# Four layers in one launch: moving comparisons of the Fourier matrices between stages

## The chip, the cores and the metric

The kernel runs on one core of a Trainium2 chip. The metric is the device time of one execution in microseconds; of several runs the median is given. Engines are named as in the profile: PE multiplies matrices (PEld loads its weights), DVE, ACT and POOL work elementwise, SP issues all transfers of this kernel.

## The reference

Four layers follow one another on x of 2048 rows and 640 columns: attention, Fourier, attention, Fourier, each added to its input after a layer norm.

```python
x = A_x
x = x + _A_ref(_layernorm(x, axis=-1), A_wqkv, A_wo)
x = x + _B_ref(_layernorm(x, axis=-1), B_dft_seq_re, B_dft_seq_im, B_dft_hid_re, B_dft_hid_im)
x = x + _A_ref(_layernorm(x, axis=-1), A_wqkv, A_wo)
x = x + _B_ref(_layernorm(x, axis=-1), B_dft_seq_re, B_dft_seq_im, B_dft_hid_re, B_dft_hid_im)
```

`_A_ref` is attention with 32 heads of 20 columns, in which a row sees itself and the 255 rows before it. `_B_ref` is the real part of a transform along the columns and along the rows:

```python
a = jnp.einsum("bsd,ed->bse", x, dft_hid_re)
b = jnp.einsum("bsd,ed->bse", x, dft_hid_im)
y = jnp.einsum("ts,bse->bte", dft_seq_re, a) - jnp.einsum("ts,bse->bte", dft_seq_im, b)
```

The four matrices are inputs.

## The kernel before, in words

All is in float32, with products of the attention's weights split into a high and a low part. The order of all instructions is fixed when the program is built; each engine takes its own in that order, and an instruction that waits holds up all behind it on its engine.

**The comparisons.** The Fourier layers use the symmetries of cosine and sine matrices and multiply only with a small part of each. That the matrices given have these symmetries is tested on the chip: 180 pieces of the four matrices (`all_checks`, L1468) are compared with their mirrored parts, and the sum of the squared differences decides at the end (`judge`, L1541, and a branch at L1719) whether a general version of the whole network is run too; with these inputs it isn't. One comparison (`check`, L1494) is a load by SP of 128 rows of 456 numbers (428 for the first 18 pieces) into a spare buffer (L1501), one or two additions or subtractions (L1508) on POOL or DVE, and a square with a sum on ACT (L1512); after every eighth, DVE adds up eight sums (L1517). A buffer is loaded again when its square is done. The comparisons have no place of their own: they are woven into the stages of the four layers.

**The stages.** Each attention has a *prologue* (`before_heads`, L411): rows are normalized and turned by PE (`prep`), the columns of V are made for 16 tiles of 128 rows (`value`, L464), and the first columns of Q and K (`pieces`). In it a comparison is loaded by `check()` and its work is put down three comparisons later (`check_step`). Five buffers, `ou` and `rr`, go round. Then come the *heads* (`heads`, L652): 128 steps, in each of which PE makes the scores and the product with V of one block of 128 rows and four heads, beside parts of the projections. In steps 0 to 80, `IN_HEADS` = 12 comparisons are spread (L875); POOL and ACT do their parts some slots after the load. The heads' step also turns the row maxima and sends them by a transfer, `qp<-mt` (L695), to the operands of the next scores.

**The Fourier layer** (`fourier`, L1314) is first a *sequence product* (the loop over `PRODUCTS`, L1368) with four comparisons to a product on DVE and ACT, and then a *column product* (L1447): eight iterations, in each of which PE multiplies one tile (`straight`), ACT copies one of the two results (L1421), DVE adds and subtracts, and PE reverses the rows of the tile before (`turned`, L1436), after which DVE adds that too and SP stores both. For the tile `j == 0` ACT copies a row into each of the two operands first (L1434). `spread(n, again)` (L1342) sets comparisons beside this: it puts the squares of the ones taken in the iteration before on ACT, loads those buffers again, and gives the POOL parts of the next n. In the second Fourier layer it takes four an iteration; in the first, none: the comparisons begun there end before the column product. Between the two products of the first layer, SP loads the weights of the second attention, five of `wv` (L378, `value_weights`) and two of `wqk` (L546, `load_chunk`); their splitting (`split_w`, L380 on ACT and L383 on POOL) is spread over the column product from its third iteration on.

Before the change the comparisons lie so: 16 in the first prologue, 12 in the first heads, 50 in the first Fourier layer, 22 in the second prologue, 12 in the second heads, 68 in the second Fourier layer.

Of the kernel before, what the change touches and what calls it, by code (L numbers as in the profile page):

```python
# [7 lines left out]
F32 = mybir.dt.float32  # L8
# [10 lines left out]
D = 640  # L19
# [31 lines left out]
PRODUCTS = [(n, c) for n in ("ce", "co", "so", "se") for c in range(3)]  # L51
SIGMA, WIDE = 513, 57
SCALED, MARGIN = 2.0 ** 40, 2.0 ** 12
IN_HEADS, CHECKED = 12, 81

CHUNKS = ((0, 16, 0, 8), (0, 16, 8, 16), (16, 24, 0, 16), (24, 32, 0, 16), (0, 32, 16, 20))

# [7 lines left out]
def cuts(ap, n):  # L65

    return [ap[:, i:i + n] for i in range(0, ap.shape[1] - n + 1, n)]
# [6 lines left out]
class Net:  # L74
    def __init__(self, nc, tc, ctx, a, ok=None):
        self.nc, self.tc, self.a = nc, tc, a
        self.general = ok is None
        const = ctx.enter_context(tc.tile_pool(name="const", bufs=1))
        self.ln = ctx.enter_context(tc.tile_pool(name="ln", bufs=5))
        self.slots = ctx.enter_context(tc.tile_pool(name="slots", bufs=1))  # L80
        psum = ctx.enter_context(tc.tile_pool(name="psum", bufs=1, space=PSUM))
        self.work = ctx.enter_context(tc.tile_pool(name="work", bufs=2))
        dram = ctx.enter_context(tc.tile_pool(name="dram", bufs=1, space=DRAM))

        self.banks = psum.tile([P, 8, 512], F32, name="banks")

        def fixed(name, cols, dt):
            return const.tile([P, cols], dt, name=name)

        self.ident = fixed("ident", P, F32)  # L90
        nc.sync.dma_start(self.ident, a["ident"])
        self.flip = fixed("flip", P, F32)
        nc.sync.dma_start(self.flip, a["flip"])
        self.mask = fixed("mask", 384, BF16)
        self.ones = const.tile([1, 128], F32, name="ones")
        nc.vector.memset(self.ones, 1.0)
        self.half = fixed("half", 1, F32)
        nc.vector.memset(self.half, -0.5)
        self.big = [None] * 4
        self.qp, self.kp = [None] * 2, [None] * 2  # L100

        self.qk = dram.tile([2, 2 * D, S], F32, name="qk_d")
        self.vd = dram.tile([NQ, P, NB, 96], F32, name="v_d")
        self.od = dram.tile([H, 32, S], F32, name="o_d")
        self.rd = dram.tile([NSB, H, 512], F32, name="r_d")
        self.xs = [dram.tile([S, D], F32, name=f"x_d{i}") for i in range(3)]
        self.turn = {}
        self.xn = {}
        self.first = True
        self.slot = None  # L110
        self.posted = {}
        self.lanes = {n: deque() for n in ("act", "dve", "pool")}
        self.heavy = []
        self.owed = {}
        self.left = 0
        self.tmp = None
        self.held = []
        self.bank_of = {}
        self.seen = fixed("seen", 2, F32)
        self.checks = deque() if self.general else deque(self.all_checks())  # L120
        self.stages = deque()
        self.n_checks = 0
        if not self.general:
            self.ok = ok
            self.ring = fixed("ring", 16, F32)
            self.part = fixed("part", len(self.checks) // 8 + 1, F32)
            self.norms = fixed("norms", 4, F32)
# [283 lines left out]
    def before_heads(self, xsrc):  # L411
        nc, a = self.nc, self.a
        self.proj = self.project()
        first = self.first
# [17 lines left out]
        def check():  # L432
            here.append(here.pop(0))
            self.check_step(here[0][:, :8 * WIDE])
# [29 lines left out]
        def value(t):  # L464
# [19 lines left out]
                                  v.rearrange("p q t c -> p q (t c)"))  # L484
            if 3 < t < 14 or t < 4 and not first:
                check()
            elif t > 13:
                for _ in range(t - 13):
                    self.check_step()
# [162 lines left out]
    def heads(self, xsrc, xdst):  # L652
# [169 lines left out]
        for step in range(-LEAD, steps + 1):  # L822
# [27 lines left out]
            for z in range(2):  # L850
# [21 lines left out]
                if z == 0 or t < -1 or t >= steps:  # L872
                    fill(nf)
                self.tick()
            if self.checks and 0 <= step < CHECKED and step * IN_HEADS // CHECKED != (step - 1) * IN_HEADS // CHECKED:  # L875
                self.check_in_heads(self.next("rr")[:, :8 * WIDE])
            if step > 16 * (NQ - 1):
                self.poll_late(step - 16 * (NQ - 1))
# [435 lines left out]
    def fourier(self, xsrc, xdst, more):  # L1314
# [9 lines left out]
        waiting = deque()  # L1324
# [68 lines left out]
        if more:  # L1393
            self.first = False
            self.value_weights()
            for c in range(2):
                self.load_chunk(c)
        temp = [[self.slot_tile(f"{n}{i}", 512, F32)[:, :HALF + 1] for n in ("vq", "rr", "ou")] for i in range(2)]
        p = self.banks[0:1, 7, :HALF + 1]
        for c in range(3):  # L1400
# [46 lines left out]
        for n, j in enumerate(order):  # L1447
            if n == 7 and not more:
                assert not self.checks and not waiting and not folded
                self.judge()  # L1450
            straight(n, j)
            if n:
                turned(n - 1, order[n - 1])
            if not more:
                spread(4, n < 5)
            if more:
                if n > 1:
                    self.split_w(3)
                if n in (2, 4):
                    self.prep_load(None, n // 2 - 1)  # L1460
                    self.prep_stats(n // 2 - 1)
                if n == 5:
                    self.prep_norm(0)
        turned(7, 6)
        if more:
            self.split_w(3 * KC)

# [255 lines left out]
```

## Time and profile before

| | |
|---|---|
| median of three runs | 1362.02 us (1356.83 to 1370.52) |
| the profiled execution | 1359.47 us |
| its span, first to last instruction | 1357.7 us |
| PE busy | 1287.9 us, 95% |
| DVE / ACT / POOL busy | 71% / 56% / 54% |
| moved by transfers | 261.50 MB, 193 GB/s on average |
| mean granted clock of PE | 0.992 |

In the profile's rows by line, "x" is a count, then come busy time and mean length, then the idle time of the engine before these instructions and what ended it. In rows in order of time the first number is the start in us from the span's start, the second the length in us, and the bracket the idle time before it with its releaser. SP's rows are issues; the transfer itself lands later. Rows by window give the length, the busy time and count of each engine, the granted clock as a share, the share of time in which the transfer engines were busy, and GB/s.

### The profile page before, as it was taken

How to read it: one execution, taken by the hardware profiler on the slowest of the kernel's cores; microseconds unless marked ns; L12 is line 12 of the kernel's file. 1: busy time of each engine (PE TensorE's matmuls, PEld its weight loads, DVE VectorE, ACT ScalarE, POOL GpSimd, SP SyncE). 2: the span in 40 equal slices, each digit the busy share in tenths (PEclk: the TensorE clock that was granted, in tenths of full speed). 3: DMA queues.
4: the chain of work that ended last, by engine and by line, in shares of the span. 5: the costliest groups of instructions: out<-in, count | busy, mean ns of one | idle time of the engine just before them, and what ended most of it. 6: DMA issues, size and time to landing. Idle time of an engine off the chain costs nothing. (4 is left out here: it accounts for less than half of the span.)

```text
span 1357.7 us, 37431 instructions
## 1 busy us (share of the span) xinstructions
PE 1287.9 (95%) x13350; PEld 992.3 (73%) x13350; DVE 967.5 (71%) x3117; ACT 765.8 (56%) x1661; POOL 735.8 (54%) x1508
## 2 busy tenths in 40 slices
PE   6999999999999889999999999999999989999997
PEld 6899777777776777753689997777777767777344
DVE  6723788887887774766866248888887868657775
ACT  3232378777776565437323325777776756744473
POOL 4221677777778674310334236787777867733044
PEclk9999999999999899999999999999999989999999
DMA  5675567777678884527536746666777788662565
GB/s 198 206 227 176 182 194 211 211 186 206 199 215 232 214 221 130 179 66 238 194 104 205 230 161 191 197 196 202 209 207 216 214 229 213 190 210 61 164 214 208
DMA packets 174298, 261.50 MB, mean 193 GB/s; under 512 B 36307, under 2 KB 85587, under 8 KB 174101
## 3 DMA queue, kind: packets, MB, share of 16 engines
q1 hardware_dynamic: 174100, 259.00, 63.7%
q8 instruction: 108, 1.77, 0.6%
q14 instruction: 90, 0.73, 0.2%
HBM read 175.42 MB, written 82.31 MB: 190 GB/s over the span
## 5 line engine op out<-in xcount | busy, mean ns | idle before, releaser
L682 DVE CUSTOM_DVE_ANT_0 banks<-banks,mask 128x384 f32<-128x384 f32 (+2 forms) x1024 | 527.1, 557 | 125.3 <-PE banks L677 107.6
L715 ACT ACTIVATE pt<-banks 128x768 f32<-128x768 f32 (+2 forms) x512 | 394.3, 772 | 147.7 <-PE banks L705 79.7
L721 POOL TENSOR_SCALAR_AFFINE_SELECT pt<-pt 128x256 f32<-128x256 f32 x512 | 224.8, 439 | 184.2 <-ACT pt L715 160.2
L275 PE MATMUL banks<-big,wc 64*128 64x512 f32 x1920 | 272.3, 394 | 0.4 <-DVE pt L481 0.4
L705 PE MATMUL banks<-qp,kp 61*128 61x384 f32 (+2 forms) x1024 | 209.6, 379 | 26.0 <-DMA qp<-mt 12.1
L677 PE MATMUL banks<-kp,qp 60*128 60x384 f32 (+2 forms) x1024 | 209.3, 353 | 5.0 <-DVE mc L682 4.6
L740 PE MATMUL banks<-pt,vq 128*32 128x128 f32 x5760 | 210.6, 277 | 0.9 <-ACT pt L715 0.8
L275 PEld LDWEIGHTS banks<-big,wc 64*128 64x128 f32 x1920 | 187.2, 185 | 22.2 <-ACT x L590 1.7
L725 POOL TENSOR_SCALAR_AFFINE_SELECT pt<-pt 128x256 f32<-128x256 f32 x448 | 187.5, 418 | 0.0
L740 PEld LDWEIGHTS banks<-pt,vq 128*32 128x32 f32 x5760 | 141.9, 109 | 48.8 <-issue 35.4
L705 PEld LDWEIGHTS banks<-qp,kp 61*128 61x128 f32 x1024 | 107.9, 184 | 88.7 <-DVE mc L682 57.8
L677 PEld LDWEIGHTS banks<-kp,qp 60*128 60x128 f32 x1024 | 124.1, 186 | 32.6 <-DVE mc L682 20.0
L682 DVE DVE_READ_ACCUMULATOR2_ANT mc<- 128x1 f32 x1024 | 144.3, 141 | 0.0
L749 ACT ACTIVATE ou<-banks 128x128 f32<-128x128 f32 (+2 forms) x288 | 73.4, 267 | 58.6 <-PE banks L740 52.2
L257 PE MATMUL banks<-qp,big 128*128 128x320 f32 x576 | 99.4, 318 | 1.0 <-POOL qp L383 1.0
L229 POOL TENSOR_TENSOR c<-x,c 128x256 fp32r<-128x256 f32 x128 | 94.9, 748 | 0.0
L257 PEld LDWEIGHTS banks<-qp,big 128*128 128x128 f32 x576 | 89.2, 193 | 1.6 <-POOL qp L383 1.4
L257 PE MATMUL banks<-qp,kp 128*128 128x320 f32 x384 | 82.2, 347 | 6.2 <-ACT big L1132 3.9
L275 PE MATMUL banks<-big,big 64*128 64x320 f32 x912 | 80.7, 313 | 0.2 <-ACT mt L693 0.2
L1508 POOL TENSOR_TENSOR rr<-rr 128x171 f32<-128x171 f32 (+3 forms) x76 | 48.3, 646 | 50.3 <-DMA rr<-hr 19.4
L257 PEld LDWEIGHTS banks<-qp,kp 128*128 128x128 f32 x384 | 61.0, 188 | 19.6 <-ACT big L1132 5.9
L275 PEld LDWEIGHTS banks<-big,big 64*128 64x128 f32 x912 | 73.7, 191 | 0.4 <-ACT mt L693 0.4
(172 smaller groups left out, 1784.2 us busy)
## 6 DMA issues: line engine op xcount, KB each, us to landing
qk_d<-c SPq DMA_DIRECT2D x80, 512.0 KB
kp<-qk_d SPq DMA_DIRECT2D x384, 80.0 KB
qp<-qk_d SPq DMA_DIRECT2D x384, 80.0 KB
o_d<-ou SPq DMA_DIRECT2D x64, 256.0 KB
v_d<-pt SPq DMA_DIRECT2D x16, 768.0 KB
vq<-v_d SPq DMA_DIRECT2D x64, 192.0 KB
kp<-ki SPq DMA_DIRECT2D x44, 228.0 KB
big<-x SPq DMA_DIRECT2D x26, 320.0 KB
```

Source lines behind the costliest of these rows:

```text
L229: eng.tensor_tensor(out=lo[..., c], in0=src[..., c], in1=hi[..., c].bitcast(F32), op=OP.subtract)
L257: self.nc.tensor.matmul(p, x, y, start=n == 0, stop=n == last)
L275: self.nc.tensor.matmul(ps[a], x[r], y[r], start=half + i == 0, stop=half == 1 and i == n - 1, skip_group_check=True)
L677: nc.tensor.matmul(p, qp[quad % 2][b:b + 60, z, qb * P:(qb + 1) * P], kp[quad % 2][b:b + 60, z, k0 * P:(qb + 1) * P], start=True, stop=True)
L682: nc.vector.tensor_tensor_reduce(out=p, in0=p, in1=self.mask[:, 384 - n * P:], scale=1.0, scalar=NEG, op0=OP.add, op1=OP.max, accum_out=mc ...
L705: nc.tensor.matmul(self.banks[:, banks[e], :n * P], kp[quad % 2][b:b + 61, z, kb * P:(kb + 1) * P], qp[quad % 2][b:b + 61, z, kb * P:(kb + ...
L715: nc.scalar.activation(pt[quad, kb][:, 2 * z:2 * z + 2, :n * P], self.banks[:, b0:b1 + 1, :n * P], AF.Exp, scale=SCALE)
L721: nc.gpsimd.affine_select(out=t[:, :, 0:P], in_=t[:, :, 0:P], pattern=[[0, 2], [1, P]], compare_op=OP.is_ge, fill=0.0, base=0, channel_mul ...
L725: nc.gpsimd.affine_select(out=t[:, :, 256:384], in_=t[:, :, 256:384], pattern=[[0, 2], [-1, P]], compare_op=OP.is_gt, fill=0.0, base=0, ch ...
L740: nc.tensor.matmul(self.banks[32 * h:32 * h + 32, bank, :P], vq[:, 96 * (kb % 4) + 21 * h:96 * (kb % 4) + 21 * h + 32], t[:, h, (qb - kb) ...
L749: nc.scalar.activation(ou[:, dst], self.banks[:, bank, src], AF.Copy)
L1508: eng.tensor_tensor(out=t[:, lo:hi], in0=t[:, lo:hi], in1=base.broadcast_to([P, hi - lo, w]), op=op)
```

## The change

`IN_HEADS` becomes a pair, 12 for the first attention and 0 for the second. In the first prologue `check()` is called twice at the tiles 5, 7, 9, 11, 12 and 13: 22 comparisons instead of 16. In the first Fourier layer six more are begun after the loads of the second attention's weights, in six parts of the buffer `big1`, and `spread` is now called in the column product of both layers, with two comparisons an iteration in the first: 14 more, 64 instead of 50. The second heads have none instead of 12, and for the second Fourier layer 60 are left instead of 68. In the new file the lines from `spread` on stand some three to six higher (L1421 is L1427, L1434 is L1440, L1436 is L1442, L1501 is L1507, L1508 is L1514, L1512 is L1518).

```diff
-IN_HEADS, CHECKED = 12, 81
+IN_HEADS, CHECKED = (12, 0), 81
...
             if 3 < t < 14 or t < 4 and not first:
                 check()
+                if first and (t % 2 or t == 12):
+                    check()
...
-            if self.checks and 0 <= step < CHECKED and step * IN_HEADS // CHECKED != (step - 1) * IN_HEADS // CHECKED:
+            share = IN_HEADS[not self.first]
+            if self.checks and 0 <= step < CHECKED and step * share // CHECKED != (step - 1) * share // CHECKED:
                 self.check_in_heads(self.next("rr")[:, :8 * WIDE])
...
             self.value_weights()
             for c in range(2):
                 self.load_chunk(c)
+            for buf in cuts(self.slot_tile("big1", 8 * D, F32), 512)[:6]:
+                begin(buf[:, :8 * WIDE])
...
-            if not more:
-                spread(4, n < 5)
+            spread(2 if more else 4, n < 5)
```

PE's instructions stand in the same order in both. On the other engines it is seen at these places.

On SP, between the two products of the first Fourier layer (`kp` takes the weights `wv`, `x` the weights `wqk`, `x_d` is the layer's result, `big` with `kr` a comparison's piece). Before:

```order
L378 DMA kp_8719<-wv 128x640 x5
L546 DMA x<-wqk 128x640 x2
L1412 DMA x_d_93<-big_6148 112x640
L1412 DMA x_d_93<-big_6148 15x640
L1412 DMA x_d_93<-big_6148 1x640
L1412 DMA x_d_93<-big_6148 128x640
L1412 DMA x_d_93<-big_6192 128x640
L1412 DMA x_d_93<-big_6148 128x640
```

Now:

```order
L379 DMA kp_8744<-wv 128x640 x5
L549 DMA x<-wqk 128x640 x2
L1507 DMA big_8756<-kr 128x456 x6
L1418 DMA x_d_93<-big_6167 112x640
L1418 DMA x_d_93<-big_6167 15x640
L1418 DMA x_d_93<-big_6167 1x640
L1418 DMA x_d_93<-big_6167 128x640
L1418 DMA x_d_93<-big_6211 128x640
L1507 DMA big_8756<-kr 128x456 x2
L1418 DMA x_d_93<-big_6167 128x640
```

Six loads of comparisons stand behind the weights and ahead of the stores, and pairs of loads among the stores.

On ACT, at the start of the column product of the first Fourier layer (`vq<-banks` of 128 rows is the copy of a tile's result, `ou<-wf` and `rr<-wf` are the row copies that the second reversal needs, `qp<-kp` splits a weight). Before:

```order
L1421 ACTIVATE vq_8734<-banks 128x321
L1439 ACTIVATE wf<-banks 1x321
L1440 ACTIVATE banks<-vq_8740 1x321
L1439 ACTIVATE wf<-banks 1x319
L1440 ACTIVATE banks<-vq_8740 1x319
L1421 ACTIVATE vq_8731<-banks 128x321
L1434 ACTIVATE ou_8736<-wf 1x321
L1434 ACTIVATE rr_8735<-wf 1x319
L380 ACTIVATE qp_8718<-kp_8719 128x640 x2
L1421 ACTIVATE vq_8734<-banks 128x321
```

Now:

```order
L1427 ACTIVATE vq_8766<-banks 128x321
L1445 ACTIVATE wf<-banks 1x321
L1446 ACTIVATE banks<-vq_8772 1x321
L1445 ACTIVATE wf<-banks 1x319
L1446 ACTIVATE banks<-vq_8772 1x319
L1518 ACTIVATE big_8756,ring<-big_8756 128x399 x2
L1427 ACTIVATE vq_8763<-banks 128x321
L1440 ACTIVATE ou_8768<-wf 1x321
L1440 ACTIVATE rr_8767<-wf 1x319
L1518 ACTIVATE big_8756,ring<-big_8756 128x399 x2
L381 ACTIVATE qp_8743<-kp_8744 128x640 x2
L1427 ACTIVATE vq_8766<-banks 128x321
```

Two squares stand ahead of the copy of the third tile and of the row copies, and two behind them; so it goes on in each later iteration.

On ACT, in the first prologue, from value tile 5 to 7 (`pt<-banks` is a value tile's copy, `big<-banks` the high part of turned rows, `ou` and `rr` with `ring` are squares). Before:

```order
L479 ACTIVATE pt_102<-banks 128x4x4x20
L1512 ACTIVATE ou_105,ring<-ou_105 128x321
L1515 ACTIVATE ou_105,norms<-ou_105 128x107
L244 ACTIVATE big_755<-banks 128x4x128
L244 ACTIVATE big_755<-banks 128x128
L479 ACTIVATE pt_103<-banks 128x4x4x20
L1512 ACTIVATE rr_106,ring<-rr_106 128x321
L244 ACTIVATE big_755<-banks 128x4x128
L244 ACTIVATE big_755<-banks 128x128
L479 ACTIVATE pt_103<-banks 128x4x4x20
L1512 ACTIVATE rr_107,ring<-rr_107 128x321
```

Now:

```order
L480 ACTIVATE pt_102<-banks 128x4x4x20
L1518 ACTIVATE ou_105,ring<-ou_105 128x321
L1521 ACTIVATE ou_105,norms<-ou_105 128x107
L1518 ACTIVATE rr_106,ring<-rr_106 128x321
L245 ACTIVATE big_758<-banks 128x4x128
L245 ACTIVATE big_758<-banks 128x128
L480 ACTIVATE pt_103<-banks 128x4x4x20
L1518 ACTIVATE rr_107,ring<-rr_107 128x321
L245 ACTIVATE big_758<-banks 128x4x128
L245 ACTIVATE big_758<-banks 128x128
L480 ACTIVATE pt_103<-banks 128x4x4x20
```

The second and the third square each come one value tile earlier.

More of the change, by code (lines that the diff above doesn't have):

```diff
@@ L122, in __init__ @@
         self.n_checks = 0
+        self.checked = 0
         if not self.general:
@@ L1464, in fourier @@
         turned(7, 6)
+        assert not waiting and not folded
         if more:
```

## The prediction

> **What bounds the kernel now.** I read the page first, then busy times by stage, then the waits of the stages that gain or lose comparisons.
>
> ```profile
> span 1357.7 us, 37431 instructions
> PE 1287.9 (95%) x13350; PEld 992.3 (73%) x13350; DVE 967.5 (71%) x3117; ACT 765.8 (56%) x1661; POOL 735.8 (54%) x1508
> ```
>
> PE is busy for 95% of the span, so the question for each stage is only what makes PE wait there. By stage (first prologue, column product of the first Fourier layer, heads of the second attention, column product of the second Fourier layer; columns are length, then busy time and count of PE, PEld, DVE, ACT, POOL, then granted clock and DMA):
>
> ```profile
> 12.00:122.00 110.00, 107.92 (x669) 102.13 (x669) 50.46 (x123) 32.44 (x95) 30.14 (x42) 1.00 0.66 204
> 643.60:680.00 36.40, 35.32 (x129) 23.98 (x129) 31.56 (x73) 14.52 (x40) 11.81 (x9) 1.00 0.51 181
> 792.60:1194.00 401.40, 386.16 (x5385) 300.81 (x5384) 316.20 (x1137) 270.71 (x527) 290.12 (x630) 0.99 0.69 201
> 1311.20:1348.70 37.50, 35.83 (x131) 23.99 (x130) 25.99 (x70) 21.54 (x71) 26.34 (x39) 1.00 0.61 210
> ```
>
> Where comparisons are taken out, PE waits little; where they are put in, PE waits hardly at all, so a gain is capped by small idle times and a loss is not capped. All terms below are changes of PE's time, since the last store follows PE's last product by a fixed chain in both kernels.
>
> **Column product of the first Fourier layer: fourteen comparisons more.** One comparison is a load, two POOL subtractions or additions (L1508) and one ACT square (L1512). In the new order SP issues the first six loads behind five loads of `wv` and two of `wqk`, POOL takes the first two at once, and ACT has their two squares ahead of its copy of the third tile (L1421) and of the two row copies (L1434). PE's reversal of the second tile (L1436) needs the first of those row copies. Before:
>
> ```profile
> 649.90 2.49 SPq L378 DMA_DIRECT2D kp<-wv  x5
> 652.44 0.91 SPq L546 DMA_DIRECT2D x<-wqk  x2
> 653.39 7.80 SPq L1412 DMA_DIRECT2D x_d<-big  x9
> 660.21 0.48 SPq L1412 DMA_DIRECT2D x_d<-big  x1
> 660.97 0.22 SPq L1412 DMA_DIRECT2D x_d<-big  x1
> ...
> SPq L1412 <- DMA x<-wqk: 0.3, 1, 0.3
> SPq L1412 <- DMA x_d<-big: 0.3, 1, 0.3
> ```
>
> The store that starts at 660.21 had waited for a landing of `wqk`, and the next, at 660.97, for that of a store. They are the 15th and the 16th transfer since 649.90, so these are the landings of the 7th and the 8th: SP runs no more than eight ahead here. The second `wqk` thus lands at about 660.2, and what stands behind it at about 660.95. In the changed kernel that 8th transfer is the first comparison's load, of similar size (by their shapes 228 against 280 KB). The next land 0.8 us apart or less. POOL and ACT then cost, by the second Fourier layer, where the same loop runs with comparisons (groups of one window of POOL, then ACT, PE and SP in order of time):
>
> ```profile
> L1508 POOL TENSOR_TENSOR kp<-kp 128x228 f32<-128x228 f32 x4 | 2.5, 625 | 0.0
> L1508 POOL TENSOR_TENSOR kp<-kp 128x171 f32<-128x171 f32 x4 | 2.0, 505 | 1.2 <-DMA kp<-ki 1.2
> ...
> 1321.79 0.52 ACT L1512 ACTIVATE kp<-kp 128x399 f32<-128x399 f32 x1
> 1322.21 0.19 ACT L1512 ACTIVATION_READ_ACCUMULATOR kp<-kp 128x1 f32 x1
> 1322.31 0.41 ACT L1421 ACTIVATE vq<-banks 128x321 f32<-128x321 f32 x1
> 1322.62 0.46 ACT L1434 ACTIVATE ou<-wf 1x321 f32<-1x321 f32 x1
> 1323.13 0.81 PE L1436 MATMUL banks<-ou,flip 128*128 128x321 f32 x2 [0.81 <-ACT ou L1434]
> ...
> 1321.80 1.88 SPq L1501 DMA_DIRECT2D kp<-ki  x4
> 1324.77 4.24 POOL L1508 TENSOR_TENSOR kp<-kp 128x171 f32<-128x171 f32 x8 [1.16 <-DMA kp<-ki]
> ```
>
> Here the same place already cost PE 0.81 us, with the data there in time. A comparison takes POOL 4.24 / 4 = 1.06 us, a square takes ACT 0.52 us (1321.79 to 1322.31), and from the copy's start to the reversal it is 0.82 us. So in the changed kernel: landing 660.95, two comparisons on POOL until 663.07, the second square until 663.59, reversal at 664.41. Before, the reversal ran without a wait:
>
> ```profile
> 654.30 1.79 PE L1420 MATMUL banks<-wf,kp 107*128 107x321 f32 x6
> 655.93 0.70 PE L1436 MATMUL banks<-ou,flip 128*128 128x321 f32 x2
> ```
>
> That is 664.41 - 655.93 = 8.5 us, nearly all of it an idle PE. The bounds: if the loads landed as fast as that of 1321.80 (2.97 us to POOL's start), the reversal would come at 653.39 + 2.97 + 2.12 + 0.52 + 0.82 = 659.82, so +3.9; if the sixth load's landing (660.95 + 5 x 0.76 = 664.75) set it, with one comparison then left on POOL, at 667.15, so +11.2. I take 8.5, since the landing of `wqk` is in the trace. Afterwards POOL has a lead: the second pair ends at 665.2 and the third at 667.3, while PE's iterations, and with them the copies that stand behind the squares, come 36.40 / 8 = 4.55 us apart. What the 14 loads do to the stores of `x_d` behind them on SP is covered: nobody reads `x_d` until the second attention's end.
>
> **The clock after that wait.** The trace has two pauses of PE in which the granted clock fell (windows of PE's pause and of what follows it, then the same eighteen matmuls at the two clocks):
>
> ```profile
> 440.98:444.38 3.40, 0.01 (x3) 0.04 (x2) 0.39 (x2) 0.85 (x3) 0.56 (x1) 0.59 0.94 285
> 444.38:448.42 4.04, 4.04 (x31) 3.59 (x35) 0.92 (x7) 1.45 (x3) 1.47 (x3) 0.50 0.87 262
> 682.94:687.40 4.46, 4.32 (x19) 4.08 (x20) 4.32 (x14) 0.77 (x2) 1.21 (x2) 0.62 0.18 59
> ...
> 444.94 2.75 PE L275 MATMUL banks<-big,big 64*128 64x320 f32 x18
> 449.56 1.48 PE L275 MATMUL banks<-big,big 64*128 64x320 f32 x18
> ```
>
> After a pause of 3.40 us the next 4.04 us ran at half clock: 4.04 x 0.50 = 2.0 us of PE's work lost; after the pause of 2.2 us before 682.94 it was 4.46 x 0.38 = 1.7. The column product is bound by PE, so a pause of eight us adds the like: I take 2.0. The low end is 0 (the next tiles' waits hide it); the high end is 3.4, if a half-clock spell as long as the one that began at 441.6 (0.41 x 3.40 x 2 = 2.8, plus 4.04 = 6.8 us) fell wholly on work.
>
> [...]
>
> **First prologue: six more.** ACT pops a square three comparisons after its load; with two in a row the load is younger when ACT comes to it. The tightest place is the square of the third comparison, now behind value tile 6 instead of 7 and ahead of ACT's split of the next transposes:
>
> ```profile
> 72.42 0.77 ACT L244 ACTIVATE big<-banks 128x512 fp32r<-128x512 f32 x2 [3.30 <-PE banks L363]
> 73.05 0.89 DVE L250 TENSOR_TENSOR big<-banks,big 128x512 fp32r<-128x512 f32 x2 [3.56 <-ACT big L244]
> 74.05 0.47 ACT L1512 ACTIVATE rr<-rr 128x321 f32<-128x321 f32 x1 [0.54 <-POOL rr L1508]
> 75.75 0.71 PE L363 MATMUL banks<-ident,x 128*128 128x128 f32 x5
> ```
>
> Its data let ACT go at 74.05, so the split at 72.42 moves to about 74.6, 2.2 us later, and DVE's part ends at 74.6 + 0.63 + 0.89 = 76.1. PE's next transposes start at 75.75 and only the fifth, some 0.4 us later, needs that bank: the cover just holds. I take +0.4; the ends are 0 and 2.2.
>
> **Heads of the second attention: twelve fewer.** This frees 12 x 1.06 = 12.7 us of POOL and 12 x 0.52 = 6.2 us of ACT, on engines that PE does not wait for. PE's waits in the steps with comparisons (827 to 1060 us):
>
> ```profile
> PE banks L705 <- DMA qp<-mt: 3.0, 2, 2.0
> PE banks L705 <- DVE mc L682: 1.9, 5, 0.6
> ```
>
> Only the two waits for a DMA can have to do with the loads. I take the shorter, 3.0 - 2.0 = 1.0 us, as the gain; the ends are -3.0 and +1.0, since transfers that shift can also meet a needed one.
>
> **Column product of the second Fourier layer: eight fewer.** The last squares now stand in the fourth iteration instead of the sixth, so ACT's copy of the seventh tile and DVE's additions come earlier, for which the verdict's matmul (L1545) waits:
>
> ```profile
> 1340.66 0.54 ACT L1512 ACTIVATE kp<-kp 128x399 f32<-128x399 f32 x1 [0.43 <-POOL kp L1508]
> 1341.20 0.42 ACT L1421 ACTIVATE vq<-banks 128x321 f32<-128x321 f32 x1
> 1342.62 0.19 PE L1545 MATMUL banks<-sums,all 128*1 128x5 f32 x2 [0.82 <-DVE ou L1408]
> ```
>
> That wait of 0.82 us goes: -0.8 (ends 0 and -1.1, with the half us lost around it). The wait of 0.81 us at 1323.13 stays, since the first four squares stay.
>
> **The sum.** 8.5 + 2.0 + 0.4 - 1.0 - 0.8 = +9.1 us. The profiled execution took 1359.47 us (its span of 1357.7 and 1.8 around it), so 1368.6; the median of the three runs, 1362.02, lies 2.6 above that execution, which would give 1371.1. I forecast from halfway between the two bases, 1360.7 + 9.1 = 1370, and count the rivals from there. Which comparison falls to which place shifts by six in the first layers; size and work stay as good as equal, and PE's own order has not changed.
>
> **The rivals.** *The loads come early.* SP's row shows the six loads queued by 656, and `big1` has been free since the sequence product. If the transfer engines served them beside the weights, the stall would be the lower bound, 3.9, with no lost clock: 3.9 + 0.4 - 1.0 - 0.8 = +2.5, 1363. Against it stands the landing at 660.2 of a transfer issued at 652.9, which was slowed by what was queued ahead. Chance 0.14.
>
> *POOL becomes the bound in the column product.* Beside DVE the same operations were slower in the second Fourier layer:
>
> ```profile
> L1508 POOL TENSOR_TENSOR kp<-kp 128x228 f32<-128x228 f32 x20 | 18.2, 911 | 0.0
> L1508 POOL TENSOR_TENSOR kp<-kp 128x171 f32<-128x171 f32 x20 | 11.1, 556 | 50.5 <-DMA kp<-ki 50.5
> ```
>
> That is 29.3 / 20 = 1.47 us for one. POOL's other work in the first layer's loop, 11.81 us by its window, falls on five iterations, 2.4 us each; with two comparisons that is 2.4 + 2.9 = 5.3 us against PE's 4.55. If ACT then waits again before each copy, it is 5 x 0.75 = 3.8 more: 9.1 + 3.8 = +12.9, 1374. Against it: POOL starts while DVE stands still. Chance 0.13.
>
> *The other side: the heads hang on POOL after all.* If each of the twelve comparisons held up mask and product behind it by its 1.06 us, the heads would give back 12.7 instead of 1.0: 9.1 - 11.7 = -2.6, 1358. It decides from a gain of 10.1 us in the heads on. Against it: PE is idle for 15.2 us in the whole 401 us of that stage, and the steps with comparisons show only the 5 us of waits quoted. Chance 0.07.
>
> That the change doesn't do what it says is no case: the new order shows all 180 comparisons, moved.
>
> **The numbers.** The stall has 0.66 and its own range is 1364 to 1374. The range 1361 to 1377 adds the early loads and most of POOL as the bound; it leaves out the heads and the tails. About 1% (13.6 us) is what this kernel's runs can tell from no change: they lie 13.7 us apart. Slower by over 1% takes half of the POOL case and the stall's upper ends with a long half-clock spell: 0.17. Faster by over 1% has no mechanism, only scatter: 0.04. Within 1%: 0.79.
>
> **What would show it.** In the changed profile: a wait of about 8 us of PE before the second reversal of the first column product (L1442 in the new numbering), released by ACT's row copy (L1440), ACT idle before a square (L1518) on POOL, and POOL idle until a DMA of `kr` lands near 661; then a granted clock of 0.50 for some us; the verdict's matmul without its wait; the steps of the second heads as long as before. The forecast is wrong if POOL's first subtraction there starts before 657, or if the heads shorten by more than 3 us.

## The result and the profile after

The changed kernel took 1371.76 us (median of 20 runs, 1363.17 to 1379.81), the kernel before, beside it on the same chip, 1364.97 (20 runs): ratio 1.0052, 95% interval 1.0033 to 1.0070, so 4.5 to 9.6 us slower. Measured once more, at the end of the study, the ratio was 1.0062 (1.0029 to 1.0095). The forecast was 1370, within 1% of the time before.

Of each of the two kernels there are two profiled executions. A stage runs here from the first PE instruction that is its own to that of the next stage; only a column product is taken to end 0.9 us after the start of its last reversal, which is 0.2 to 0.6 us behind the first instruction of the next stage (lengths in us, worked out from the traces):

| stage | before | again | changed | again |
|---|---|---|---|---|
| start and first prologue | 122.4 | 123.5 | 125.5 | 124.8 |
| first heads, with what follows them | 468.7 | 468.4 | 470.1 | 466.8 |
| sequence product | 50.8 | 50.8 | 50.9 | 50.9 |
| column product | 38.7 | 38.7 | **49.6** | **48.7** |
| second prologue | 112.0 | 110.5 | 111.6 | 110.4 |
| second heads, with what follows them | 466.1 | 465.1 | 463.2 | 463.0 |
| sequence product | 50.8 | 50.8 | 54.1 | 50.8 |
| column product | 39.6 | 39.3 | 38.8 | 38.8 |
| end | 8.6 | 8.2 | 7.8 | 7.9 |
| span | 1357.7 | 1355.4 | 1371.6 | 1362.0 |

The page of the first profile after begins so:

```profile
span 1371.6 us, 37440 instructions
PE 1296.1 (94%) x13350; PEld 996.2 (73%) x13350; DVE 971.3 (71%) x3123; ACT 766.3 (56%) x1661; POOL 734.0 (54%) x1502
```

PE does the same 13350 matmuls in 8.2 us more than before (1296.1 against 1287.9), so part of the loss is a slower clock and the rest idle time. The idle time lies in the column product of the first Fourier layer: PE is idle there for 8.7 of 49.64 us, and before the change for 1.1 of 38.68. Of the 8.2 us, 3.3 lie there too (40.92 us busy against 37.60), and another 3.4 in a stretch of half clock in the second sequence product (the second row below), which the second profile of the changed kernel does not have. The view of busy times by window (the whole stage; a stretch of the second sequence product; the second column product; the stretch behind the first stage's wait):

```profile
646.44:696.08 49.64, 40.92 (x140) 26.60 (x139) 33.49 (x80) 22.86 (x70) 28.48 (x37) 0.90 0.57 201
...
1285.45:1292.28 6.83, 6.83 (x9) 2.02 (x9) 4.67 (x16) 3.02 (x10) 0.00 (x0) 0.50 0.24 74
1325.02:1363.78 38.76, 37.49 (x137) 24.40 (x136) 26.98 (x74) 16.80 (x55) 18.62 (x24) 1.00 0.49 172
...
668.23:674.47 6.24, 6.24 (x12) 4.05 (x13) 3.88 (x11) 3.11 (x9) 6.24 (x10) 0.50 0.71 237
```

The first stage's 49.64 us hold only 40.92 of PE, at a granted clock of 0.90. SP, POOL, ACT and PE in order of time show why:

```profile
654.69 2.23 SPq L379 DMA_DIRECT2D kp<-wv  x5
656.96 0.91 SPq L549 DMA_DIRECT2D x<-wqk  x2
657.91 4.68 SPq L1507 DMA_DIRECT2D big<-kr  x6
...
664.70 6.83 POOL L1514 TENSOR_TENSOR big<-big 128x171 f32<-128x171 f32 x12 [65.70 <-DMA big<-kr]
665.83 0.54 ACT L1518 ACTIVATE big<-big 128x399 f32<-128x399 f32 x1 [7.00 <-POOL big L1514]
...
667.72 0.46 ACT L1440 ACTIVATE ou<-wf 1x321 f32<-1x321 f32 x1
...
668.23 1.44 PE L1442 MATMUL banks<-ou,flip 128*128 128x321 f32 x2 [7.36 <-ACT ou L1440]
```

POOL waits for the load of `kr`, ACT waits 7.00 us with a square for POOL, the row copy stands behind two squares, and PE waits 7.36 us for it. From the stage's start (646.44) the reversal comes at 21.79 us; before the change it came at 14.00 (655.93 less 641.93). That is 7.8 us. The reversal itself, the six matmuls behind it and two more then run at half clock, 6.24 us in all, which loses 3.1. Together that is 10.9 of the 11.0 us by which the stage grew.

### The profile page after: what moved, and what is told of

It is laid out like the page before. It is cut to its first block, busy times and chain, and to the rows that moved or that the text cites. A ratio compares the mean times of both kernels' runs of the same rounds, so it can differ in the third digit from the quotient of the medians.

```text
span 1371.6 us, 37440 instructions
## 1 busy us (share of the span) xinstructions
PE 1296.1 (94%) x13350; PEld 996.2 (73%) x13350; DVE 971.3 (71%) x3123; ACT 766.3 (56%) x1661; POOL 734.0 (54%) x1502
## 5 line engine op out<-in xcount | busy, mean ns | idle before, releaser
L258 PE MATMUL banks<-pt,big 128*128 128x320 f32 x384 | 67.5, 311 | 0.0
```

The source lines that it names most:

```text
L258: self.nc.tensor.matmul(p, x, y, start=n == 0, stop=n == last)
```

## Experiments

Each ratio is to the kernel before, run beside it on the same chip, with its 95% interval. No kernel leaves work out unless its expectation says so.

### The parts alone

The column part alone is the changed kernel with these two edits; "column and heads" has the second edit alone.

```diff
-IN_HEADS, CHECKED = (12, 0), 81
+IN_HEADS, CHECKED = (12, 12), 81
...
-                if first and (t % 2 or t == 12):
-                    check()
```

> The column part alone: fourteen comparisons in the first Fourier layer's column product, taken from the second Fourier layer (54 there instead of 68); first prologue (16) and second heads (12) as before. Nothing is left out. Theory A (the wait for the loads behind the weights is what the change costs): column product of the first layer 38.7 us before, +10 to +12 here, of it a wait of 7 to 8 us of PE ahead of the second reversal, released by ACT's row copy, POOL's first subtraction not before 660 on the trace's own time less any shift of the earlier stages, granted clock 0.50 for 7 to 11 us; second Fourier column product -1 to -2 (fourteen fewer); total +9 to +10.5 against before, ratio 1.0065 to 1.0077. Theory B (the stall is partly made by the six comparisons of the first prologue, which shift what falls there): stage less than +8, total +5 to +7, ratio 1.004 to 1.005.

> Column part and heads: as the column part alone, but the twelve comparisons of the second heads go to the second Fourier layer (66 there). Against the column part alone it isolates the heads. Theory A (only waits for transfers of the sums' mt and of masks go, PE waits for little else): heads of the second attention -2 to -3 us against the column part alone, second Fourier column product +1 (twelve more), together -1 to -2, so about +7.5 to +9 against before, ratio 1.0055 to 1.0066. Theory as put in the prediction: heads -1.0, so no difference that the clock of the runs can show. Rival (heads hang on POOL): -10 or more, total near 0.

The prologue part alone keeps the first edit, has the six comparisons in the prologue, and leaves the column product without any:

```diff
-            for buf in cuts(self.slot_tile("big1", 8 * D, F32), 512)[:6]:
-                begin(buf[:, :8 * WIDE])
...
-            spread(2 if more else 4, n < 5)
+            if not more:
+                spread(4, n < 5)
```

> The prologue part alone: 22 comparisons in the first prologue, second heads (12) as before, none in the column product of the first Fourier layer, 62 in the second Fourier layer. Nothing is left out. Theory A (the pair of loads at value tile 13, behind which the odd one's square stands in ACT ahead of the copies of the last transposes): a wait of PE of about 2 us near 122, released by ACT's copy into pt (L480), POOL waiting 7 to 8 us for the load of kr before it; prologue +2.4 to +3.4; second Fourier column product -0.4; total +2 to +3, ratio 1.0015 to 1.0022. Theory as put in the prediction: +0.4 in the prologue, at ACT's split near 72, no wait near 122, ratio 1.000 within 0.0007.

Measured: column part 1.0082 (1.0051 to 1.0112), with the heads 1.0051 (1.0022 to 1.0079), prologue part 1.0035 (1.0013 to 1.0056). The stall is there with or without the six comparisons of the prologue. PE's rows in order of time, of the column part and then of column and heads:

```profile
670.97 1.44 PE L1440 MATMUL banks<-ou,flip 128*128 128x321 f32 x2 [8.12 <-ACT ou L1438]
```

```profile
663.60 1.44 PE L1440 MATMUL banks<-ou,flip 128*128 128x321 f32 x2 [8.05 <-ACT ou L1438]
```

The column product took 48.7 and 49.1 us, so +10.0 and +10.4: theory A. Against the column part alone, column and heads tests the heads: their stage takes 462.6 us against 465.7, -3.1 where -2 to -3 was expected. But all of that comes behind the steps that hold comparisons, above all at a wait of PE for `qp<-mt` in step 102 (1.27 us against 4.08). Two things were not expected. In the second Fourier layer's column product, where I expected a gain, the column part alone lost 3.5 us and the prologue part 4.3 (43.1 and 43.9 us against 39.6). The prologue part's rows in order of time there:

```profile
1315.16 11.38 POOL L1513 TENSOR_TENSOR kp<-kp 128x171 f32<-128x171 f32 x16 [47.80 <-DMA kp<-ki]
1315.54 1.19 DVE L1513 TENSOR_TENSOR kp<-kp 128x171 f32<-128x171 f32 x4
...
1318.43 1.38 DVE L1513 TENSOR_TENSOR rr<-rr 128x171 f32<-128x171 f32 x2
...
1323.63 1.38 DVE L1513 TENSOR_TENSOR ou<-ou 128x171 f32<-128x171 f32 x2
...
1327.34 1.44 PE L1440 MATMUL banks<-ou,flip 128*128 128x321 f32 x2 [4.03 <-DVE ou L1412]
```

While POOL works on its comparisons, DVE's last ones take 1.38 / 2 = 0.69 us each instead of 1.19 / 4 = 0.30, and PE waits 4.03 us. In this profile the place costs 4.3 us, and the start and prologue some 1.7 (124.7 against 123.0 on average with 16 comparisons). But the profiled execution lay 5.0 us above the median of its twelve, and POOL and DVE meet at this place in every profile: DVE's comparisons are slowed in these two and, in part, with the heads, and not in the eleven others (see the last section). So how the 1.0035 of the median is made up, and whether the place's price belongs to the prologue part, isn't shown. The prologue's own wait is there, as theory A had it:

```profile
122.34 1.58 PE L258 MATMUL banks<-qp,big 128*128 128x320 f32 x9 [1.16 <-ACT pt L480]
```

### The loads ahead of the weights

```diff
+            for buf in cuts(self.slot_tile("big1", 8 * D, F32), 512)[:6]:
+                begin(buf[:, :8 * WIDE])
             self.value_weights()
             for c in range(2):
                 self.load_chunk(c)
-            for buf in cuts(self.slot_tile("big1", 8 * D, F32), 512)[:6]:
-                begin(buf[:, :8 * WIDE])
```

> The changed kernel with one move: the loads of the six first comparisons of the column product are issued ahead of the weights' loads (wv, wqk) instead of behind them. Nothing is left out. Theory A (the stall is the landing of these loads behind seven weights): SP issues them near 644, while it stood idle until 654.7; POOL's first subtraction by 650, no wait of PE of more than 1 us before the second reversal, granted clock 1.00 through the stage, column product 38.7 to 40.5 us instead of 49.6; total -9 to -11 against the changed kernel, so -2 to -4 against before, ratio 0.997 to 0.9985. Rival (POOL's and ACT's work for fourteen comparisons binds the stage, whenever the data come): a wait of 3 us or more moves to a later iteration, total no better than +3 against before, ratio 1.002 or more.

Measured: 1.0032 (1.0011 to 1.0053); column product 44.8 us, between the two theories; the total is the rival's (1.002 or more). The wait behind the weights is gone, and another has come, one reversal earlier. In order of time:

```profile
640.77 2.70 SPq L1507 DMA_DIRECT2D big<-kr  x6
...
643.56 8.42 POOL L1514 TENSOR_TENSOR big<-big 128x171 f32<-128x171 f32 x12 [53.59 <-DMA big<-kr]
643.59 0.64 DVE L1514 TENSOR_TENSOR ou<-ou 128x171 f32<-128x171 f32 x2
...
648.36 2.67 DVE L1514 TENSOR_TENSOR kp<-kp 128x171 f32<-128x171 f32 x4
...
653.36 1.44 PE L1442 MATMUL banks<-ou,flip 128*128 128x321 f32 x2 [4.20 <-DVE ou L1414]
```

POOL now works while DVE still has the last comparisons of the sequence product, whose operations go from 0.64 / 2 = 0.32 to 2.67 / 4 = 0.67 us. ACT's squares of these comparisons of DVE stand ahead of its copies for the column product, and DVE needs such a copy for what PE waits for. A second theory, then: POOL's subtractions slow DVE's. Its test keeps the early loads and the squares:

```diff
+        gate = [0]
...
-                one()
-                two()
+                if not more or gate[0] >= 6:
+                    one()
+                    two()
+                gate[0] += more
```

> The run with the six loads ahead of the weights, but the subtractions and additions on POOL of those first six comparisons in the column product are left out (their squares then sum raw values, so the verdict is not the reference's); loads and squares stay. Theory A (POOL's twelve operations run beside DVE's last comparisons of the sequence product and slow them, 0.67 us each instead of 0.32, and the first reversal's wait of 4.20 us hangs on these): DVE's comparisons keep 0.32 us each to their end, the wait is 0.6 to 1.3 us, column product 39 to 41 us. Rival (the wait comes from the transfers or the order on ACT): the wait stays at 3.5 us or more, column product 43.5 or more. Total by A -3 to -5 against the run with the early loads.

Measured: the total says nothing here (4044.61 us, since the false sums make the general version run too), but the stage is as the theory had it: column product 39.0 us, DVE at 1.19 / 4 = 0.30 us to its end, and the wait back to 1.36:

```profile
650.97 1.19 DVE L1517 TENSOR_TENSOR kp<-kp 128x171 f32<-128x171 f32 x4
654.49 0.81 PE L1445 MATMUL banks<-ou,flip 128*128 128x321 f32 x2 [1.36 <-DVE ou L1417]
```

So loads and squares of fourteen comparisons cost the stage next to nothing if the data are there, and the six that run beside DVE's last comparisons cost 5.8 us (44.8 less 39.0, with the half clock behind the wait) by being done on POOL.

### Filling the pause

```diff
+            if more and n == 2:
+                for _ in range(24):
+                    nc.tensor.matmul(self.banks[:, 2, :HALF + 1], wc[0][:107, :P], wc[0][:107, :], start=True, stop=True)
```

> The changed kernel with 24 products more, of 128 columns by 321, whose result nobody reads, between PE's last product ahead of the wait in the first column product and the reversal that waits (24 x 0.27 = 6.5 us of the pause of 7.4 us). Nothing is left out, the added products are idle work. Theory A (the pause halves the clock): granted clock 1.00 behind the wait, the six matmuls behind the reversal in 1.79 us instead of 3.42, column product 46 to 47 us instead of 48.7 to 49.6; total -2.5 to -3.5 against the changed kernel, ratio to before 1.002 to 1.004. Rival (what is long behind the pause has another cause, such as traffic of transfers): the six matmuls stay at 3 us or more, column product 49 or more, no gain.

> As the run with the 24 added products, whose 48 matmuls took 13.12 us, but with 12 of them: 24 matmuls of 0.273 us, 6.56 us, inside the pause. Nothing is left out, the added products are idle work. Theory A (the pause halves the clock and that costs 2 to 3.4 us): the reversal comes as early as in the changed kernel (PE's idle time and the added products together 7 to 8 us), no spell of half clock behind it, column product 46 to 47 us against 48.4 to 49.6, ratio to before about 0.002 below that of the changed kernel in this call. Rival (the added products themselves hold up what follows, or the clock falls all the same): 48.4 us or more, no difference from the changed kernel.

With 24 products: 1.0087 (1.0054 to 1.0120). My size was wrong: a product of these operands is two matmuls, so the 24 were 48 matmuls and took 13.12 us, and the reversal started at 668.71 although ACT's row copy had started at 662.66. The six matmuls behind the reversal took 1.79 us, as the six ahead of the added products. With 12, PE in order of time, and then the whole stage by window:

```profile
655.31 6.64 PE L1460 MATMUL banks<-wf 107*128 107x321 f32 x24
662.78 0.81 PE L1442 MATMUL banks<-ou,flip 128*128 128x321 f32 x2 [0.83 <-ACT ou L1440]
663.43 0.70 PE L1442 MATMUL banks<-rr,flip 128*128 128x319 f32 x2
663.97 1.79 PE L1426 MATMUL banks<-wf,qp 107*128 107x321 f32 x6
```

```profile
641.00:687.60 46.60, 44.41 (x164) 29.40 (x163) 32.55 (x80) 23.35 (x70) 28.35 (x37) 1.00 0.60 214
```

The reversal waits as long as ever, but behind it six matmuls take 1.79 us, and the stage 46.5 us instead of 48.4 to 49.6: theory A, the half clock costs 2 to 3 us of the stage. The whole time, 1.0072 (1.0049 to 1.0095), shows no gain over the changed kernel beside it (1.0062); its runs are few (6), and two or three us are at the edge of what they can tell.

### Starting in the third iteration

```diff
-                if first and (t % 2 or t == 12):
+                if first and t in (5, 7):
...
-            spread(2 if more else 4, n < 5)
+            if n > 1 or not more:
+                spread(2 if more else 4, n < 5)
```

> The changed kernel, but the pairs of comparisons in the first Fourier layer's column product start in its third iteration instead of its first (10 of them instead of 14); first prologue 18 (doubled behind value tiles 5 and 7 only), second heads 0, second Fourier layer 68 as before. Nothing is left out. The loads stay behind the weights. Theory A (a square that stands in ACT ahead of a copy costs only what its load lacks; by the third iteration the loads have landed): no wait of PE above 1.1 us in the stage, granted clock 1.00 there, column product 38.7 to 40 us against 48.7 to 49.6 in the three kernels with fourteen; heads of the second attention 462.3 to 463.3 as in the others without comparisons there; total -2 to -5 against before, ratio 0.9963 to 0.9985. Rival (POOL's and ACT's work for comparisons binds the stage): column product 43 us or more, total +1 or more, ratio above 1.0005.

The stage went as theory A had it: 39.4 us with ten comparisons in it and a clock of 1.00. The stage by window, and its second reversal, without a wait, in order of time:

```profile
644.30:683.69 39.39, 37.31 (x136) 24.53 (x136) 31.80 (x79) 20.36 (x60) 21.49 (x27) 1.00 0.63 227
```

```profile
658.33 0.70 PE L1442 MATMUL banks<-ou,flip 128*128 128x321 f32 x2
```

The total was not as expected: 1.0022 (1.0001 to 1.0043) where 0.9963 to 0.9985 was expected. In its profile both sequence products are longer, by 5.0 and 3.3 us, at half clock (see below), and the second prologue takes 113.0 us instead of 110.4 to 112.0, with a pause of 2.77 us at its start that was 2.17 before. The half clock can be chance, the longer second prologue came again in the next run (113.8 us, with the same pause of 2.77 us). What keeps the median of twelve executions from the gain is not settled by one profile. The same kernel with PE's pause in the heads filled:

```diff
+                    if (t, z) == (102, 0):
+                        for _ in range(10):
+                            nc.tensor.matmul(self.banks[:, banks[0], :P], self.flip, self.flip, start=True, stop=True)
                     t_pair(t // 16, t % 16, z, banks)
```

> The kernel whose comparisons start in the third iteration of the column product, with ten products of 128 by 128 more in each attention (idle work, 20 matmuls, by estimate 2.2 us), ahead of the pair of products in step 102 of the heads, where PE pauses 2.4 to 4.8 us in the kernel before, the changed one and the variants, with 3.4 to 10.2 us of half clock behind. Nothing is left out. [...]

Measured: 1.0004 (0.9980 to 1.0029), the same as the kernel before, so no version here beats it. The two windows around step 102, without the products and then with them:

```profile
434.00:452.00 18.00, 13.04 (x176) 11.20 (x174) 9.65 (x38) 8.69 (x18) 11.47 (x21) 0.81 0.88 267
1105.00:1125.00 20.00, 16.59 (x227) 13.43 (x227) 11.88 (x41) 11.42 (x21) 13.11 (x24) 0.83 0.83 255
```

```profile
434.00:452.00 18.00, 16.01 (x200) 13.46 (x196) 10.52 (x38) 9.16 (x19) 11.68 (x21) 0.91 0.86 267
1105.00:1125.00 20.00, 17.61 (x254) 14.60 (x247) 13.32 (x47) 11.85 (x22) 14.04 (x27) 1.00 0.76 218
```

The clock stays at 1.00 in the second attention, where 20.00 us at 0.83 had been 0.17 x 20.00 / 0.50 = 6.8 us of half clock; in the first a spell of 3.41 us remains, which began at 438.88, ahead of the products. Yet the heads grew shorter by only 0.3 and 0.4 us. In the first attention the products themselves ran mostly at half clock, took 3.86 us (2.50 in the second) and held the next pair up to 443.20, where it had come at 441.94 without them; in the second nothing held it up, and where the gain went is not settled.

### The prologue, and both kernels again

```diff
-IN_HEADS, CHECKED = (12, 0), 81
+IN_HEADS, CHECKED = (12, 2), 81
...
-                if first and (t % 2 or t == 12):
+                if first and t % 2 and t < 12:
```

> The changed kernel with four instead of six more comparisons in the first prologue, behind value tiles 5, 7, 9 and 11 only (none at 12 and 13); the two go to the second heads (2 there), second Fourier layer 60 as in the changed kernel. Nothing is left out. Theory A (the price of the prologue is the young square of the last pairs, ahead of ACT's copies into pt): PE's wait near 120 to 123 (2.13 us in the changed kernel, 1.16 with the prologue part alone, 1.51 with the early loads) is below 0.5; load and first prologue together 1 to 2 us shorter than the changed kernel's 125.5; the rest as in the changed kernel, column product 48.7 to 49.7, total -1 to -2 against it, ratio to before 1.004 to 1.0045. Rival (the added loads or POOL's work slow the whole stage): the wait moves elsewhere in the prologue, no gain.

Measured: 1.0074 (1.0048 to 1.0101), not the -1 to -2 us of theory A in the total. In the profile PE's wait near 121 is gone and start and prologue take 123.5 us. The end of the prologue in order of time, first in the changed kernel and then, PE alone, in this one:

```profile
114.74 1.79 SPq L643 DMA_DIRECT2D qp<-qk_d  x5
116.64 0.36 SPq L1507 DMA_DIRECT2D rr<-kr  x1
...
120.91 0.95 POOL L1514 TENSOR_TENSOR rr<-rr 128x399 f32<-128x399 f32 x1 [7.84 <-DMA rr<-kr]
121.81 0.95 POOL L1514 TENSOR_TENSOR ou<-ou 128x399 f32<-128x399 f32 x1
121.89 0.54 ACT L1518 ACTIVATE rr<-rr 128x399 f32<-128x399 f32 x1 [8.22 <-POOL rr L1514]
...
122.65 0.41 ACT L480 ACTIVATE pt<-banks 128x320 f32<-128x320 f32 x1
...
123.12 1.14 PE L258 MATMUL banks<-qp,big 128*128 128x320 f32 x6 [2.13 <-ACT pt L480]
```

```profile
119.04 1.48 PE L258 MATMUL banks<-qp,big 128*128 128x320 f32 x9
120.36 1.04 PE L258 MATMUL banks<-pt,big 128*128 128x320 f32 x6
121.24 1.48 PE L258 MATMUL banks<-qp,big 128*128 128x320 f32 x9
```

> The kernel before, unchanged, for a second profile of it and as a measure of what the comparison itself scatters: ratio 1.000 within 0.002. In the changed kernels a spell of half clock with no pause of PE fell into 8 of 18 sequence products, 11 to 15 us after their start; the kernel before had none in its two. [...] Column product of the first layer 38.7 us within 0.5, first prologue with its load 122 to 123.5.

> The changed kernel, unchanged, on the same chip as the three others of this call. Ratio to before 1.003 to 1.007, as measured. Theory A: column product 48.4 to 50 us with a wait of 6.5 to 8 us ahead of the second reversal and a spell of half clock behind it; PE's wait for the copy into pt near 121 of 1.2 to 2.2 us; the DVE operation of 4.8 us near 307 was a single event and is not there, first heads 465 to 469 us; second heads 462 to 464. Rival for the prologue (the wait near 122 was a single event as well): below 0.5.

Measured: the kernel before 0.9991 (0.9966 to 1.0017) against itself, the changed one 1.0062. The changed kernel's column product is 48.7 us, with a wait of 7.08 us at the second reversal; the wait for the copy into `pt` is there with 0.95 us; its first heads took 466.8, so the single late operation of the first profile (below) was one event. The kernel before again had no half clock in its sequence products. (Its expectation counts 8 such spells in 18 products; the traces had 7.)

## Why the prediction was right, step by step

**Column product, +8.5 and clock, +2.0: right, and each a little off.** The mechanism is the one forecast, at the place forecast and with the releasers named: the loads behind seven weights, POOL, two squares, row copy, reversal. The reversal came later by 7.8 us in the first profile; from their stages' starts the same sum gives 7.5 (the changed kernel again), 8.3 (column part), 8.2 (with heads) and 6.6 (four in the prologue). The clock term was mis-sized the other way: half clock for 6.24 us behind the wait, 3.1 instead of 2.0, near its upper bound of 3.4. The stage grew by 9.7 to 11.0 in these five profiles, against 10.5 by the sum. Three runs bear the mechanism out: with the loads ahead of the weights this wait is gone (another came in its place), with the pause filled the half clock is gone, and with the start in the third iteration ten comparisons fit in without either.

**First prologue, +0.4: wrong place, and too small.** At ACT's split near 72, which I took for the tightest place, PE's wait stayed without effect. The wait came at the end, where the load that belongs to tile 12 is issued only at 116.64, behind the transfers of `qk_d`, lands when POOL has waited 7.84 us for it, and its square stands ahead of ACT's copy into `pt`. All seven profiles with 22 comparisons there have it, 0.95 to 2.13 us, and none of the seven with 16, 18 or 20. Start and prologue together take 124.4 us on average in six of these (the run that leaves subtractions out is not counted), and 123.0 in the four with 16: +1.3, within the bound of 2.2.

**Second heads, -1.0: right sign, too small, and right only in part by the reason given.** They take 463.1 us on average in seven profiles without comparisons (those with products added in the heads or subtractions left out are not counted), and 466.0 in the four with twelve: -2.9, at the bound of -3.0. The two waits on which the term rested are in two of the four profiles with twelve comparisons (3.0 and 2.1 us, so 1.3 on average) and in none of four others (the changed kernel twice, column and heads, twelve products in the pause). About 2.0 us more lie in a stretch behind all the comparisons, some 287 to 326 us into the stage, where PE pauses at step 102: it takes 40.2 us on average in the four, with 6.83 us of half clock in each, and 38.2 in the seven, with 0 to 6.83. The single values touch (39.3 to 41.4 against 35.4 to 39.3), so whether taking the comparisons out shortens this stretch, or chance does, isn't shown.

**Second column product, -0.8: right.** 38.8 us in both profiles against 39.6 and 39.3; the verdict's matmul no longer waits.

**The sum.** With the measured sizes, 10.5 + 1.3 - 2.9 - 0.8 = +8.1; the two comparisons of the times gave +6.8 and +7.1, the forecast was +9.1. An under-sized gain and an under-sized loss in part made up for each other. That the forecast of 1370 lies within 2 us of 1371.76 is luck as well: its base, 1360.7, lay 4.3 below the 1364.97 that the kernel before took beside the changed one, and its loss of 9.1 lay 2.3 above the measured 6.8. Of the rivals, the early loads did not happen (POOL's first subtraction came 18.3 us into the stage, the forecast was 19.0); POOL did not become the bound (behind that wait PE waits nowhere in the stage for more than 0.15 us; the 1.47 us for one comparison on which that rival rested is a mean with one operation of 5.22 us in it, and without that it is about 1.2); the heads did not hang on POOL (twelve comparisons by 1.06 would have given -12.7). The one rival I did not think of is what the early loads brought out: POOL against DVE.

## What to carry to other kernels

Background work spread into a gap cost here what its data lacked when ACT reached it in its order: ACT stood 7.00 us at a square, and PE 7.36 us for the copy behind it. So look at what is queued ahead of its load, and start it some iterations later (a stage of 39.4 us) before moving the load earlier (44.8). A single profile of each kernel was good for the place of a loss of ten microseconds, not for sums of terms below three: look at each stage over several profiles.

## What the runs showed of the hardware

**POOL and DVE beside one another: one of them was slower.** In the column product with the early loads, DVE's 0.30 to 0.32 us for a comparison's operation became 0.67 beside POOL's subtractions, and with these left out it stayed at 0.30; at the second column product of the prologue part it became 0.69. It is not always DVE that is slowed. At the start of the second column product DVE has sixteen such operations left and POOL begins its own, in all 14 profiles. In 11 of them DVE keeps its 0.30 us and one operation of POOL lasts 5.07 to 5.38 (0.505 and 0.625 are the means of these operations in the window that the prediction quotes); only in the column part, the prologue part and, later on, column and heads is DVE slowed. Why one slows the other, and what decides which, no run shows. The changed kernel, POOL and DVE in order of time:

```profile
1325.23 5.38 POOL L1514 TENSOR_TENSOR kp<-kp 128x171 f32<-128x171 f32 x1 [50.86 <-PE banks L1316]
...
1325.73 1.19 DVE L1514 TENSOR_TENSOR kp<-kp 128x171 f32<-128x171 f32 x4
```

The long operation can be DVE's, too. In the changed kernel's first profile one DVE operation lasted 4.81 us under a row of short POOL operations, and PE waited for DVE. The other 27 of its group took (23.2 - 4.8) / 27 = 0.68 us each. Its group, and then the place in order of time:

```profile
L230 DVE TENSOR_TENSOR wc<-x,wc 128x384 fp32r<-128x384 f32 (+1 forms) x28 | 23.2, 840 | 0.0
```

```profile
307.17 4.81 DVE L230 TENSOR_TENSOR wc<-x,wc 128x384 fp32r<-128x384 f32 x1
...
309.43 0.73 POOL L230 TENSOR_TENSOR c<-x,c 128x256 fp32r<-128x256 f32 x1
...
310.83 0.73 POOL L230 TENSOR_TENSOR c<-x,c 128x256 fp32r<-128x256 f32 x1
...
312.30 0.33 PE L680 MATMUL banks<-kp,qp 60*128 60x128 f32 x2 [3.52 <-DVE mc L685]
```

**The clock fell with no pause at all.** In the sequence products six matmuls with one row (`1x512`) alternate with full ones. PE in order of time, where the clock was halved at 1285.45 (1.00 over the 3.03 us before, 0.50 over the 6.83 us after, PE busy throughout):

```profile
1282.42 1.10 PE L1315 MATMUL banks<-wf,vq 1*107 1x512 f32 x2
1283.45 1.11 PE L1316 MATMUL banks<-big,pt 128*107 128x512 f32 x2
1284.49 1.12 PE L1315 MATMUL banks<-wf,vq 1*107 1x512 f32 x2
1285.54 2.04 PE L1316 MATMUL banks<-big,pt 128*107 128x512 f32 x2
```

All spells of half clock between a trace's start and its end are multiples of 3.413 us long (3.413, 6.827 and 10.240 us in the first profiles of the two kernels), so I laid stretches of that length from their edges over the 28 sequence products of the 14 profiles. In the seven where the clock fell, 3.0 to 3.5 us behind the first such matmul, one stretch held 2.35 to 2.52 us of one-row matmuls, their lengths added up (2.37 in the rows above); in the 21 others none held more than 2.30. That was found afterwards in these same traces, and no run changed these matmuls, so what halves the clock there is not shown. The product took 3.3 us more where it fell, once 5.0. The kernel before has the same matmuls; in its four sequence products the clock stayed at 1.00.
